# Holding activation loads back, under a new stored order, so that the first weights have the DMA engines alone, in a linear-attention plus gated-MLP kernel

## Chip, cores, metric

One core of one Trainium2 chip. The metric is device microseconds of one execution, median over the runs of a comparison, in which the kernel before runs on the same chip in the same rounds. The record calls an execution slow when a lower granted clock goes with a longer time, or when it is over 1.5% above the fastest of its kernel. Each trace is one execution.

## The reference

```python
h   = x + A(layernorm(x))          # linear attention: qkv = x @ wqkv, phi(q), phi(k), kv, o = num / den, o @ wo
h2  = h + B(layernorm(h))          # gelu(x @ w_in) in halves z1, z2; w_sp mixes layernorm(z2) over tokens; (z1 * g) @ w_out
# S = 2048 tokens (16 tiles of 128), D = 512, 32 heads; w_sp is 2048 x 2048; everything bf16
```

Mostly the opening matters here: layernorm of x by tiles of 128 tokens, transposition of the normalised tile (xn to xnT), the key product, the feature map (written pk), and the accumulation of pk with xn over all tokens. Later the normalised h (hn) is transposed by the DMA to hnT. In the profiles PE is TensorE, DVE is VectorE, ACT is ScalarE, POOL is GpSimd and SP is SyncE; a q behind the name (SPq) is the queue from which that engine issues its DMA transfers.

## The kernel before

The kernel records every operation with its dependencies and then emits them per engine in a **stored order** (`ORDER`, a packed list). The stored order decides how instructions stand on every engine; waits follow from the data.

```python
    x0 = load_x("SP", 0, 1, 2150)
    load_x("ACT", 1, 1, 2250)
    x2 = load_x("SP", 2, 1, 2500)
    load_x("ACT", 3, 1, 2500)
    wk = [first_load(eng, wqkv[:, c:c + 2, D:2 * D], ..., f"wk{c}", 3500)      # key weights, 2 x 256 KB
          for eng, c in (("SP", 0), ("ACT", 2))]
    for n, lat, behind in ((4, 3900, None), (6, 3500, x0), (8, 3600, x2), (10, 3300, wk[0]), (12, 3500, wk[0]),
                           (14, 3700, wk[0])):
        load_x("SP", n, 2, lat, behind)                                        # 256 KB each; behind = wait for that load
    first_load("SP", wqkv[:, :, 0:D], A_wqkv[:, 0:D], "wq", 4500)              # query weights, 512 KB
    # ... cut ...
    # tiles 0 to 5 are transposed by TensorE (HEAD = 6), tiles 6 to 15 by the DMA from SP:
            if n < HEAD:
                pe_transposes(xn[:, i, :], b + i % 2, xnT, i, second)
            else:
                g.last = dma_t(xnT[:, :, i * P:(i + 1) * P], xn[:, i, :], f"xt{i}")
                if i == HEAD:
                    first_xt = g.last
    # ... cut: w_sp, loaded transposed from HBM. The first of its tiles (EARLY = 1) goes ahead of all the xnT transposes:
        w = NT // 2 if EARLY <= i < NT // 2 else NT
        for j in range(0, NT, w):
            op = dma_t(wsp[:, j:j + w, t * P:(t + 1) * P], B_w_sp[...], ...)
            op.soft.add(queue["SP"][-1].i if i < EARLY else prev.i)
            prev = op if i >= EARLY else prev
            if i < EARLY:
                first_xt.soft.add(op.i)
```

So SP's queue reads: x0, x2, wk, x4 to x14, wq, one transposed w_sp load (512 KB), then the xnT transposes. No w_sp tile is used before about 120 us.

Of the kernel before, what the change touches and what calls it, by code (L numbers as in the profile page):

```python
# [11 lines left out]
P = 128  # L12
GRAN = 16
EARLY = 1
SEM_NS = 45.0
ORDER = "c-jrogMttU00qE@tj)G<d$VoZwz=81ZQHhO+jiZ}FH8U;Aqt`)I$|IuVj(u-pq}C*0RSQ#Lc$1!;0TQ{2mv8HA|f)PA}*335t1S?k|8-#ASH4k4{{?fQXwDmqYx^h0Mep7Dxm@zp$Xz4AyT6-(x3=3pdiwr7&0L}0+A6#kr|EA6qQj0&Cnbz(E?SG1zC{|HIN;}(G}fM0zJ?TB~cAIP#rZ<8*NYvtxyVeP#0rR8f7pJV=*4}P#;UM6wA;SIZ+nn&>pSP4n5Heeb5`B5CLH^0TVF^lhGdo&=>tM1s%`;4KWA<F%5&!5zEmD2XP385riQ)f)!YaRalLqIEE8Aj^P-Abr^{?IE_&ljj5Q9&gg=fn1T6NfLS<+g;<ZZIE6EKhUa*R7kG-<n1i7hh7H(=MOchY*n#cXj4hapdDw%!*oj@(jdM7Qeb|o!*otkqiYqve3%H0&xQWZShFiFf8+eUZc!RgNjeEF{JGhGn2+oHH!H|r=06s!QzQcPw#uNO+Cw#yUe8gvb!7qHpH^ks~{6S3q`@g)t8Ym1yF)Twf79%qfqcAGtF*f5e4#P7Xe<Ky6F*P$Y53?{j^D;jRFb&f(9n&)dGcps+tRxFEA4{<`|3b{h?99QO3}hh|W)T);E(T*w)?ryDU^&KTLM~wo7Gnw4Wi2LR875|VR$xU|VoTOzZB}L#)@K7YWFt1_V&>)=u4QZXVs}<$b+%z|E@fM`ViPuF4>nYBmSl1!WfCT13Z`Uo?co-tP*3h<A1>n*4rOY!V|#YsKCa__PGw3pWi{4db2d^MrP6vH;4pS%CoX4Su3$fQ<py?Uf3D;J4&)#PF}*S<tuiZ}wlbrpa|APKII}3LvTGZ&DW`HMmvSqwy0EcEas~&p8;7uonyQ(atA$#smGUT`@~fZ<sE`6xSfe<NGg(B%bcRJ$Ld8`|C3TjiRYpg6ly`WAcX^C&SWZ{@gxC0%<yBTs`G<e`j9>Vb-?*KlxskKDgF88!b2yjtxQSypmg6{{tGJ5?xsVe$pVxVuhj@dNc#rRRj^}xwhk28?c$=Gff+zW&7x;nCd5RzTf-m`r-}#UK_v!(E@F5p*0Vi`JE2)CQtD+*PvRW&d+NiDCsl7U=qdKXxx~PhRD}(~{nX9>*5%rT7`HQdkn~x|x=4n<_JXKXl#a9j0RCOiLYhGd~MN&dtW;8`tBE^suT45Ack(F3U6h*-lQ?Zm(;S^P|6-RN^Uv*SVGqg&*)kgy~NK-UeGgVhXnysPgs^RLU?pmu68mQG8qG1}Pahk4?nyT^Yrw!_%zUrxITBie=pt+i*(dwmn8l(AIpoJQ%Ihv?RO5({{qNQ4-Wm>O|+N{OeqHU_J<=U<_+N7;op_SU9ojRx#-m4SZrG473BRZ<%I;oUCrFcH9LprV9+M_f2pks>fq&}y!I<H*5pi8=<)K1{*x~6o#sLQ&etGcUOx~Y50?Sy`ykNT|p`lMt|<VSj_w0^8-dZHIf<yU&G41TKTdZ{n^s&{&;^!}#r`k};5<1EhVU;3$x{;hxdBl@rMI=O>6o9#@7<<Jh}0uJdA4(rSg=kU(&07r0kM|2biI+`Onvhz5HV>qYtIjW;OjtjZ43%aO_IHpUun2Wov>$#yDxuj#ev75N5OS`#yx|f@|tjoBCd%M2-x`F$+rCYhb`?<B-xUC0xpa*%d%ejJsJk&$n&J|tB<z3lTT-~KS!BsuclU>7;T+_8&&9&X$9o*5w-N~KZ#ob-UQ#{qvJj@%t$(udWBRtD9Jl&(c#oav0<2=?gy~eXW$Md|_>pa&ByvR$u-t)cCi@ns#z09k;(%Zb<JG|336w1N<UT+lFU42_y9m``p-aWj*E4<pf{2yF?$Zh"


class _Op:
# [13 lines left out]
class _Prog:  # L33
# [110 lines left out]
    def schedule(self):  # L144

        ids = np.frombuffer(zlib.decompress(base64.b85decode(ORDER)), np.uint16).tolist()
        assert len(ids) == len(self.ops)
# [105 lines left out]
def bass_sequential_preLN__linear_attn_block__mixer_gmlp__prompt_kernel(  # L253
# [11 lines left out]
    _, S, D = A_x.shape  # L265
    F = B_w_in.shape[1]
    FH = F // 2
    H = 32
# [9 lines left out]
    g = _Prog(nc)  # L278
# [37 lines left out]
    TB, SB = HT * GW * 2, HT * P * 2  # L316
# [3 lines left out]
    x = g.sbuf("x", o_x, [NT, D], BF16)  # L320
    h = g.sbuf("h", o_x, [NT, D], BF16)
    xn = g.sbuf("xn", o_xn, [NT, D], BF16)
    wqkv = g.sbuf("wqkv", o_wqkv, [KD, 3 * D], BF16)
# [19 lines left out]
    m = g.sbuf("m", o_m, [KD, D], BF16)  # L343
# [125 lines left out]
    wq = A_wqkv.rearrange("(c p) f -> p c f", p=P)  # L469
    queue = {"SP": [], "ACT": []}  # L470

    def load(eng, dst, src, nm, lat, issue=500.0):
        return dma(eng, dst, src.rearrange("(c p) f -> p c f", p=P), nm, lat=lat, issue=issue)

    def first_load(eng, dst, src, nm, lat, behind=None):
        q = queue[eng]
        op = load(eng, dst, src, nm, lat)
        op.bias = 1e6
        if q:
            op.soft.add(q[-1].i)  # L480
        if behind is not None:
            op.deps.add(behind.i)
        q.append(op)
        return op

    def load_x(eng, n, w, lat, behind=None):
        return first_load(eng, x[:, n:n + w, :], x_d[n * P:(n + w) * P, :], f"x{n}", lat, behind)
# [4 lines that stand above are left out]
    load_x("ACT", 3, 1, 2500)  # L492
    wk = [first_load(eng, wqkv[:, c:c + 2, D:2 * D], A_wqkv[c * P:(c + 2) * P, D:2 * D], f"wk{c}", 3500)
          for eng, c in (("SP", 0), ("ACT", 2))]
    for n, lat, behind in ((4, 3900, None), (6, 3500, x0), (8, 3600, x2), (10, 3300, wk[0]), (12, 3500, wk[0]),
                           (14, 3700, wk[0])):
        load_x("SP", n, 2, lat, behind)
    first_load("SP", wqkv[:, :, 0:D], A_wqkv[:, 0:D], "wq", 4500)
    exp_table = g.add("ACT", lambda ac: ac.preload_act_table_set("natural_log_exp_and_others"), [], [], cost=1300)
    exp_table.soft.add(queue["ACT"][-1].i)  # L500
    exps = []
# [104 lines left out]
    def next_pair():  # L606
        pc[0] += 1
        return PAIRS[pc[0] % 2]
# [118 lines left out]
    for c in range(KD):  # L727
        b = CB[1 - c % 2]
# [15 lines left out]
    for tg in range(NG):  # L744
# [12 lines left out]
        if tg not in MERGE:  # L757
# [3 lines left out]
            for t in range(first, tg + 1):  # L761
                for c in range(0, KD, 2):
                    q, r = pqT[:, c:c + 2, t * GW:(t + 1) * GW], r16[t // 2][:, c:c + 2, t % 2, :]
# [8 lines left out]
    for n in range(NT):  # L772
        b = AB[n % 3]
        matmuls(bank(b), [(pqT[:, c, n * P:(n + 1) * P], m[:, c, :]) for c in range(KD)])
        s = st[1][:, n, :]
# [20 lines left out]
    for n in range(NT):  # L796
        b = next_pair()
# [12 lines left out]
        s = st3[:, n, :]  # L810
# [18 lines left out]
    k = 0  # L829
    for tg in range(NG):  # L830
        for fc in range(KF):
            b = Z1B[k % 2]
# [6 lines left out]
    for i, t in enumerate(order):  # L839
        w = NT // 2 if EARLY <= i < NT // 2 else NT  # L840
# [12 lines left out]
    v1, v2, v3, v4 = (rows(0, HF, hi, half) for hi in (0, 1) for half in (0, 1))  # L853
# [166 lines left out]
```

## Time and profile before

| | |
|---|---|
| median | 233.85 us (3 runs, 233.68 to 233.93) |
| TensorE (PE) | busy 224.1 of 232.1 us, 89% of the chain that ended last |
| where PE is idle | mostly the first 19 us, some between 48 and 67 us |
| key weights | issued at 1.72, landed 5.8 us later |
| w_sp load | issued at 9.49, landed 8.5 us later, at 17.96 |
| first xnT by DMA | issued at 14.70, landed 3.8 us later, at 18.5 |

The page of the kernel before, its first part and its chain:

```profile
span 232.1 us, 3230 instructions
PE 224.1 (97%) x1180; PEld 110.4 (48%) x1203; DVE 159.8 (69%) x323; ACT 103.8 (45%) x193; POOL 45.0 (19%) x134
...
PE 89%; DVE 3%; DMA 3%; POOL 2%; issue 1%; ACT 1%; SPq 1%; DVEq 0%
```

PE bounds the kernel, and so anything that moves its dense stretch moves the end. The chain of waits of the kernel before, cut to the opening (start us, us, what):

```profile
2.19 6.07 DMA x<-in_A_x_dram
...
8.29 0.69 DVE st L511
8.98 0.64 DVE xn L556 x2
...
16.25 1.29 PE psum L655 x6
17.54 0.05 issue
17.60 1.24 PE psum L655 x5
18.84 1.73 PE psum L402 x8
```

The chain waits 6.07 us for x4, then passes through VectorE; from 12.9 us on it stays on PE. The timeline of the kernel before (start us, us, engine, line, operation, out<-in, count, and the idle time before with its releaser):

```profile
6.40 0.41 DVE L556 TENSOR_SCALAR xn<-x,st,rs 128x512 bf16<-128x512 bf16 x1 [0.31 <-ACT rs L421]
8.29 0.69 DVE L511 BATCH_NORM_STATS2 st<-x 128x6 f32<-128x512 bf16 x1 [1.47 <-DMA x<-in_A_x_dram]
8.90 0.72 DVE L556 TENSOR_SCALAR xn<-x,st,rs 128x512 bf16<-128x512 bf16 x2
...
9.91 2.75 PE L402 MATMUL psum<-wqkv,xnT 128*128 128x512 bf16 x12
...
18.68 1.89 PE L402 MATMUL psum<-wqkv,xnT 128*128 128x512 bf16 x8
20.40 1.89 PE L655 MATMUL psum<-pk,xn 128*128 128x512 bf16 x8
...
8.98 0.47 SPq L432 DMA_DIRECT2D wqkv<-in_A_wqkv_dram  x1
9.49 4.94 SPq L435 DMA_TRANSPOSE wsp<-in_B_w_sp_dram  x1
```

Two norms (8.90) wait for x4 only because the statistics of x4 stand in front of them on VectorE. The products at 18.68 are those of tiles 6 and 7, the first that use an xnT made by the DMA; the products of pk and xn at 20.40 (L655) are called the next group below. The DMA view of the kernel before (bytes of one issue, us from issue to landing):

```profile
wqkv<-in_A_wqkv_dram SPq DMA_DIRECT2D x1, 256.0 KB, 5.8
x<-in_A_x_dram SPq DMA_DIRECT2D x1, 256.0 KB, 6.1
...
wqkv<-in_A_wqkv_dram SPq DMA_DIRECT2D x1, 512.0 KB, 5.6
wsp<-in_B_w_sp_dram SPq DMA_TRANSPOSE x1, 8.5
...
xnT<-xn SPq DMA_TRANSPOSE x1, 3.8
```

The table of windows of the kernel before (stretch, us, busy time of each engine, granted clock, DMA share, GB/s):

```profile
2.00:9.00 7.00, 5.13 (x54) 4.12 (x53) 3.69 (x10) 4.78 (x12) 2.18 (x8) 1.00 0.84 262
9.00:17.00 8.00, 7.40 (x45) 3.38 (x46) 7.97 (x24) 6.32 (x11) 3.63 (x10) 1.00 1.12 243
```

The DMA share is the time of all packets over that of the 16 engines (packets that overlap can bring it above 1): 0.84 from 2 to 9 us and 1.12 from 9 to 17 us; by single microseconds it is 0.34 from 8 to 9 us.

### The profile page before, as it was taken

The numbers are of one execution on the slowest core, as the hardware profiler recorded it, in microseconds if no ns is written. First come the engines' busy times: TensorE is split into PE (matmuls) and PEld (weight loads), VectorE is DVE, ScalarE is ACT, GpSimd is POOL, SyncE is SP. The second block draws the span as 40 slices with busy tenths as digits, with TensorE's granted clock in tenths as the row PEclk, the third lists the DMA queues.
The fourth block names the chain that finished last, engine by engine and source line by source line (L and its number), as shares of the span: only waits on it lengthen the run. The fifth ranks groups of instructions, "written<-read, shape, count | busy, mean of one in ns | idle before, by whom it ended". The sixth has DMA issues, their size and how long they took to land.

```text
span 232.1 us, 3230 instructions
## 1 busy us (share of the span) xinstructions
PE 224.1 (97%) x1180; PEld 110.4 (48%) x1203; DVE 159.8 (69%) x323; ACT 103.8 (45%) x193; POOL 45.0 (19%) x134
## 2 busy tenths in 40 slices
PE   7699999999999999999999999999999999999995
PEld 7344444453344443455444444444455555555453
DVE  3699855637898820129679996688797695582595
ACT  5586654389869687689762010112111212013110
POOL 3354300000665500726851000000000000000000
PEclk9999999999999999999999999999999999999999
DMA  6894339937457469939999300000000002000015
GB/s 189 262 206 91 57 60 336 340 72 182 110 98 156 95 131 146 186 78 212 176 226 222 73 3 0 0 0 0 3 0 24 0 3 90 0 24 3 0 45 181
DMA packets 58864, 23.68 MB, mean 102 GB/s; under 512 B 48480, under 2 KB 58720, under 8 KB 58848
## 3 DMA queue, kind: packets, MB, share of 16 engines
q1 hardware_dynamic: 58144, 22.88, 44.8%
q10 hardware_dynamic: 704, 0.59, 0.8%
q8 instruction: 9, 0.15, 0.3%
q14 instruction: 7, 0.06, 0.1%
HBM read 7.47 MB, written 2.10 MB: 41 GB/s over the span
## 4 chain that ended last, share of the span: by engine, by line
PE 89%; DVE 3%; DMA 3%; POOL 2%; issue 1%; ACT 1%; SPq 1%; DVEq 0%
PE psum L402 70%; PE psum L655 6%; PE psum L802 6%; PE psum L805 4%; DMA x<-in_A_x_dram 3%; DVE st L511 1%; POOL rs L551 1%; PE psum L751 1%; SPq L432 1%; ACT m L421 0%; POOL st L535 0%; PE psum L720 0%; PE psum L676 0%; DVE xn L556 0%; PE psum L685 0%
## 5 line engine op out<-in xcount | busy, mean ns | idle before, releaser
L421 ACT ACTIVATE psum<-psum 128x256 f32<-128x256 f32 (+1 forms) x33 | 14.4, 445 | 91.6 <-PE psum L402 42.5
L402 PE MATMUL psum<-wsp,z 128*128 128x512 bf16 x203 | 47.1, 379 | 0.3
L402 PEld LDWEIGHTS psum<-wsp,z 128*128 128x128 bf16 x208 | 20.3, 98 | 23.1 <-ACT psum L421 0.5
L402 PE MATMUL psum<-hnT,win 128*128 128x512 bf16 x109 | 25.3, 379 | 0.2
L402 PE MATMUL psum<-t,s 128*128 128x512 bf16 x94 | 22.2, 379 | 0.1
L421 ACT ACTIVATE e<-psum 128x1024 bf16<-128x1024 f32 (+1 forms) x18 | 16.7, 927 | 12.5 <-PE psum L402 12.0
L421 ACT ACTIVATE z1T<-psum 128x512 bf16<-128x512 f32 x28 | 16.3, 594 | 4.9 <-PE psum L402 4.9
L924 DVE TENSOR_TENSOR u<-psum,bsp 128x512 bf16<-128x512 f32 x16 | 11.0, 687 | 10.2 <-PE psum L402 7.5
L421 ACT ACTIVATE z<-psum 128x896 bf16<-128x896 f32 x16 | 14.5, 914 | 4.1 <-PE psum L805 4.1
L402 PEld LDWEIGHTS psum<-hnT,win 128*128 128x128 bf16 x112 | 9.9, 98 | 13.5 <-ACT z1T L421 4.1
L402 PE MATMUL psum<-wout,z1T 128*128 128x256 bf16 (+1 forms) x82 | 16.3, 314 | 0.0
L802 PE MATMUL psum<-win,hnT 128*128 128x512 bf16 x63 | 16.2, 379 | 0.1
L402 PE MATMUL psum<-wqkv,xnT 128*128 128x512 bf16 x62 | 14.9, 379 | 0.9 <-ACT xnT L421 0.8
L556 DVE TENSOR_SCALAR hn<-h,st,rs 128x512 bf16<-128x512 bf16 x16 | 6.0, 407 | 13.7 <-POOL rs L547 13.2
L402 PE MATMUL psum<-xnT,wqkv 128*128 128x512 bf16 x61 | 15.1, 379 | 0.2
L655 PE MATMUL psum<-pk,xn 128*128 128x512 bf16 x63 | 15.2, 379 | 0.1
L402 PE MATMUL psum<-m,pqT 128*128 128x512 bf16 x62 | 14.7, 379 | 0.4 <-DVE h L776 0.3
L402 PEld LDWEIGHTS psum<-t,s 128*128 128x128 bf16 x96 | 9.4, 98 | 10.4
L511 DVE BATCH_NORM_STATS2 st<-x 128x6 f32<-128x512 bf16 x15 | 9.9, 677 | 5.0 <-DMA x<-in_A_x_dram 5.0
L776 DVE SCALAR_TENSOR_TENSOR h<-psum,x 128x512 bf16<-128x512 f32 x16 | 10.5, 682 | 4.0 <-PE psum L402 4.0
L805 PE MATMUL psum<-win,hnT 128*128 128x384 bf16 x64 | 13.0, 326 | 0.0
L582 DVE TENSOR_SCALAR e<-e 128x1024 bf16<-128x1024 bf16 (+1 forms) x18 | 7.0, 391 | 7.9 <-ACT e L421 7.7
(113 smaller groups left out, 348.6 us busy)
## 6 DMA issues: line engine op xcount, KB each, us to landing
r<-rcp SPq DMA_DIRECT2D x16, 128.0 KB, 2.7
out_dram<-h SPq DMA_DIRECT2D x15, 128.0 KB, 1.8
win<-in_B_w_in_dram SPq DMA_DIRECT2D x2, 896.0 KB, 8.6
x<-in_A_x_dram SPq DMA_DIRECT2D x6, 256.0 KB, 4.8
wqkv<-in_A_wqkv_dram SPq DMA_DIRECT2D x2, 512.0 KB, 8.6
wout<-in_B_w_out_dram SPq DMA_DIRECT2D x1, 896.0 KB, 8.0
wo<-in_A_wo_dram SPq DMA_DIRECT2D x1, 512.0 KB, 4.1
bsp<-in_B_b_sp_dram SPq DMA_DIRECT2D x1, 512.0 KB, 4.8
```

The source lines that it names most:

```text
L402: inst = pe.matmul(out_ap, lhsT=a, rhs=b, start=start and i == 0, stop=stop and i == len(pairs) - 1, **kw)
L421: return g.add("ACT", lambda ac: ac.activation(out_ap, in_ap, func, **kw), [in_ap, *extra], [out_ap] + ([accum] if accum is not None else []),
L432: return g.add(eng, lambda q: q.dma_start(out_ap, in_ap), [in_ap], [out_ap], cost=issue, lat=lat, dma=name, **k)
L511: dve(lambda v: v.bn_stats(s[:, 0:6], src[:, n, :]), [src[:, n, :]], [s[:, 0:6]], D)
L551: pool(lambda p: p.tensor_tensor(r, ve, expo[:, 0:1], ALU.pow), [ve, expo], [r], 620)
L556: return dve(lambda v: v.tensor_scalar(dst, src, mean, rst, op0=ALU.subtract, op1=ALU.mult), [src, mean, rst], [dst], w + 460, acc=4)
L582: dve(lambda v: v.tensor_scalar(e, e, 1.0, EPS_PHI, op0=ALU.min, op1=ALU.add), [e], [e], w * GW, acc=4)
L655: inst = pe.matmul(bank(CB[c]), lhsT=xn[:, i, c * P:(c + 1) * P], rhs=pk[:, i, :], start=i == 0, stop=i == NT - 1)
L776: dve(lambda v, n=n, b=b, s=s: v.scalar_tensor_tensor(h[:, n, :], bank(b), 1.0, x[:, n, :], op0=ALU.mult, op1=ALU.add, accum_out=s[:, 0:1] ...
L802: pe.matmul(bank(b), lhsT=hnT[:, c, n * P:(n + 1) * P], rhs=win2[:, c, 0:GW], start=c == 0, stop=c == KD - 1)
L805: inst = pe.matmul(bank(b + 1, F2), lhsT=hnT[:, c, n * P:(n + 1) * P], rhs=win2[:, c, GW:FH], start=c == 0, stop=c == KD - 1)
L924: dve(lambda v: v.tensor_tensor(t, bank(b), add, ALU.add), [bank(b), add], [t], GW, ps=True)
```

## The change

Intent: x4 and x6 wait for the landing of x2, and x8 to x14 for that of the key weights, so that the key weights do not share the DMA engines. The stored order was made anew for the new arrival times, so every engine's order differs.

```diff
-ORDER = "c-jrogMttU00qE@tj)G<d$VoZwz=81ZQHhO+jiZ}... (cut)"
+ORDER = "c-jTQ17HvU00h8Cwq47%ZQHhO+qGrewr$(CZ5wwH5gA... (cut)"
...
-    for n, lat, behind in ((4, 3900, None), (6, 3500, x0), (8, 3600, x2), (10, 3300, wk[0]), (12, 3500, wk[0]),
-                           (14, 3700, wk[0])):
+    for n, lat, behind in ((4, 2000, x2), (6, 2200, x2), (8, 1900, wk[0]), (10, 2100, wk[0]), (12, 2300, wk[0]),
+                           (14, 2500, wk[0])):
         load_x("SP", n, 2, lat, behind)
-    first_load("SP", wqkv[:, :, 0:D], A_wqkv[:, 0:D], "wq", 4500)
+    first_load("SP", wqkv[:, :, 0:D], A_wqkv[:, 0:D], "wq", 3400)
```

The change has two parts: **the hold** (the `behind` entries; the latencies are only estimates of the scheduler and change no instruction) and **the schedule** (`ORDER`).

More of the change, by code (lines that the diff above doesn't have):

```diff
@@ L15 @@
 SEM_NS = 45.0
-ORDER = "c-jrogMttU00qE@tj)G<d$VoZwz=81ZQHhO+jiZ}FH8U;Aqt`)I$|IuVj(u-pq}C*0RSQ#Lc$1!;0TQ{2mv8HA|f)PA}*335t1S?k|8-#ASH4k4{{?fQXwDmqYx^h0Mep7Dxm@zp$Xz4AyT6-(x3=3pdiwr7&0L}0+A6#kr|EA6qQj0&Cnbz(E?SG1zC{|HIN;}(G}fM0zJ?TB~cAIP#rZ<8*NYvtxyVeP#0rR8f7pJV=*4}P#;UM6wA;SIZ+nn&>pSP4n5Heeb5`B5CLH^0TVF^lhGdo&=>tM1s%`;4KWA<F%5&!5zEmD2XP385riQ)f)!YaRalLqIEE8Aj^P-Abr^{?IE_&ljj5Q9&gg=fn1T6NfLS<+g;<ZZIE6EKhUa*R7kG-<n1i7hh7H(=MOchY*n#cXj4hapdDw%!*oj@(jdM7Qeb|o!*otkqiYqve3%H0&xQWZShFiFf8+eUZc!RgNjeEF{JGhGn2+oHH!H|r=06s!QzQcPw#uNO+Cw#yUe8gvb!7qHpH^ks~{6S3q`@g)t8Ym1yF)Twf79%qfqcAGtF*f5e4#P7Xe<Ky6F*P$Y53?{j^D;jRFb&f(9n&)dGcps+tRxFEA4{<`|3b{h?99QO3}hh|W)T);E(T*w)?ryDU^&KTLM~wo7Gnw4Wi2LR875|VR$xU|VoTOzZB}L#)@K7YWFt1_V&>)=u4QZXVs}<$b+%z|E@fM`ViPuF4>nYBmSl1!WfCT13Z`Uo?co-tP*3h<A1>n*4rOY!V|#YsKCa__PGw3pWi{4db2d^MrP6vH;4pS%CoX4Su3$fQ<py?Uf3D;J4&)#PF}*S<tuiZ}wlbrpa|APKII}3LvTGZ&DW`HMmvSqwy0EcEas~&p8;7uonyQ(atA$#smGUT`@~fZ<sE`6xSfe<NGg(B%bcRJ$Ld8`|C3TjiRYpg6ly`WAcX^C&SWZ{@gxC0%<yBTs`G<e`j9>Vb-?*KlxskKDgF88!b2yjtxQSypmg6{{tGJ5?xsVe$pVxVuhj@dNc#rRRj^}xwhk28?c$=Gff+zW&7x;nCd5RzTf-m`r-}#UK_v!(E@F5p*0Vi`JE2)CQtD+*PvRW&d+NiDCsl7U=qdKXxx~PhRD}(~{nX9>*5%rT7`HQdkn~x|x=4n<_JXKXl#a9j0RCOiLYhGd~MN&dtW;8`tBE^suT45Ack(F3U6h*-lQ?Zm(;S^P|6-RN^Uv*SVGqg&*)kgy~NK-UeGgVhXnysPgs^RLU?pmu68mQG8qG1}Pahk4?nyT^Yrw!_%zUrxITBie=pt+i*(dwmn8l(AIpoJQ%Ihv?RO5({{qNQ4-Wm>O|+N{OeqHU_J<=U<_+N7;op_SU9ojRx#-m4SZrG473BRZ<%I;oUCrFcH9LprV9+M_f2pks>fq&}y!I<H*5pi8=<)K1{*x~6o#sLQ&etGcUOx~Y50?Sy`ykNT|p`lMt|<VSj_w0^8-dZHIf<yU&G41TKTdZ{n^s&{&;^!}#r`k};5<1EhVU;3$x{;hxdBl@rMI=O>6o9#@7<<Jh}0uJdA4(rSg=kU(&07r0kM|2biI+`Onvhz5HV>qYtIjW;OjtjZ43%aO_IHpUun2Wov>$#yDxuj#ev75N5OS`#yx|f@|tjoBCd%M2-x`F$+rCYhb`?<B-xUC0xpa*%d%ejJsJk&$n&J|tB<z3lTT-~KS!BsuclU>7;T+_8&&9&X$9o*5w-N~KZ#ob-UQ#{qvJj@%t$(udWBRtD9Jl&(c#oav0<2=?gy~eXW$Md|_>pa&ByvR$u-t)cCi@ns#z09k;(%Zb<JG|336w1N<UT+lFU42_y9m``p-aWj*E4<pf{2yF?$Zh"
@@ new lines @@
+ORDER = "c-jTQ17HvU00h8Cwq47%ZQHhO+qGrewr$(CZ5wwH5gAbt9Wf9Su@D<^5Eu2800D@ED2Rr5$b~$}jl4*LqyUHz2nE3iiC_qhWJrz_NQp#9j8w>n{3w9JNQ(-ngvO|hifD@XNQl%(gMui6bjW~0NROh(gp4SL;;4eE$c!dvhAgOttSEtOsEO>Tj&A6I?kI_#D23)|fpBPrmgt4v=!-tcfm*16wy2FdXpPdSi+UJ`GAN7sXn-*oi}6^7B{+=bSc-PYiE=294rqh+XoyA_fPol{e&~-u=!i}@g3dUILzsYxn1sn#foYh6Ay|pf2#+ubi&cn#)i{b{IDz9BieU)ENCaUNMq>@uVLGOw3%X(^W?%v4<1|iU78YVH*5eGG;uKz@fg0)sp5qy2V-AL61U6tJ7GW`VU^_NpGqzwZ=3x)^VkdTCH_qWK_F+E`U@Nxa3a;WjF5n_A;U+HQ8gAh_Zr~N(;5FXjHtypN?&2OEA~+u)1Vi#2BJdF+G7{h8F`nQjKHvvF;uk*QAHLu-zTqprBPPMH49!ps!&o$9Gb*DoGNUja<1-H9G91J6H)1dqQ!@`UGdlA!3-hx8(=aX5F+DRdBQvoaOS2ZqeEfr~EJ*P$$}kwSF*|cGCkwGWb1{GkSeQjvl*L$=3Au#z*pj)~gSA<lCE13Fn3xr~m}Oa?OIe4l*qXiBmVH=}l~|co*p6$smJQgDjaZfK*^@Qcm`&J=eVLTWS%RgQgvq#t$(4dlnUc-9hbgp-TbWvEG@MgdjoUbaBiWA~*pZ#sp99#L138Gxxt%+>f-5<d={22=)L1pSjx(4+d%2HY*p1EDg4LN)sgzl1704hC<zRMaR}SM4Hc=L(Q$~$qCQai^o?%vHQ+DN0PUTiE<y9W#S3VU`K^0aZ713E9VR02z2^CXml~fs(S1Fa%9UkQ|-sKg(;Z>H?6TW2y&EkF@;6bkE25#hNj^S92<4*44A&%#4&f#3H;yg~^ah~9OF63cO;wEn9J>KU7KIBQB;yb?Q2cF}3Uf@OU=4r0xHD2c>HdQk<R|~aND^2DCPUIq1RAp7tA3o(X{$&+a)fawcHHBAeB~u%<RXep;2X#~@bygR3RRn!waD`A!g;Xtl<a6HOO+MlazT_>w;wS!NL|x`<J|+}NRAhbU5B}sY-e!CyP!xqyXh~rdRbgcXD4~8ckrFG3s;h>gD~3KZreZ0!!YP`PDvshRnBr-G`e?9ftFC6Kj%I3zhN_+hs;_2ixVmYIrfQJ7tG{|^l~!w-rYle*HCMybQzO(*qclz%G+MnBr16@ddFrkC8lzd7sC8PPC0eMpO5(Aaqyw6xrCOuOTBh~dsLfiWE!wJs+NPvltP@(U?b@Xk+N71*p}jh+L)xvK+Nb?GqCGmQ<4Wk0I;GP(qeMQY#LnfjI;RvquM4`QD@y5$itl8;rcb)A54x<Yx}&?grJK5^+`g{|O6>#=@JBt;L#6U#J<|(4(Nm@MXT8=drE_{e*B8CiS7q=!z125;*AFFk7XQ*uW%O_T6a7bjmEXZ^!*XbcabAaX2#0lehjSWda#m+{HWzR~M{q<(avn!@WJh-t7jkw-a|{=DKF4t^$8-+obP*SIF_&>!7k3HQbA88kBR6&vH*hmIbxD_ULr-!GH+OlrbSw9A8~1h}w{}IBb|qK#1o!hq_jP{{a67kkdk^#=5AiTp@nBbVIoEInS95jObS>9*M|bu{*Ku8UcMnhTR8MmUZ}Mgj^(+r}Cy(?DPxlsg@np|*kViPsvpvsqJl6}n$V)um3%%G&J<g-u)nmQfqrA+kywYpD*6SSG!F@yV+|!}F)$jF2x7E#KyxJ=~-s`==+q~U7ywkh<AMVe{ZU"
```

## The prediction

> **What bounds the kernel now.** TensorE: busy 224.1 of 232.1 us (first part of the page), 89% of the chain that ended last, granted clock 1.00. Its idle time lies almost wholly in the first 19 us and between 48 and 67 us (timeline of PE, table of windows).
>
> In the opening the chain of waits reads: x load until 8.29 us, statistics of x4 on VectorE, then norms. The x4 load was issued at 2.19 and took 6.1 us to land; the key weights, issued at 1.72, took 5.8 to 6.0 (landing 7.5 to 7.8); x8, issued near 4.06, took 5.6. So 0.5 MB of weights shares the DMA engines with up to 0.75 MB of x not needed yet. The Trainium skill (DMA: Bandwidth & Descriptors, "Two DMAs through the same engine are not ordered") says descriptors start in order but are pipelined; the trace agrees that being early in the queue did not land the weights quickly.
>
> The weights are not the tight wait, though: the first key product is released at 7.83 by ScalarE's copy of xnT. What costs most is VectorE's order: the statistics of x4 stand before the norms of x3 and x1, which so wait until 8.98, although their inputs were ready by about 7.2. TensorE idles for it at 7.27 to 7.86, 8.89 to 9.35, 12.66 to 12.91.
>
> **What changes.** x4 and x6 wait for x2 (landed about 4.06), x8 to x14 for the first key weights. No bytes or arithmetic are added. The stored schedule is replaced whole: in the opening the norms of tiles 0 to 3 come before the statistics of x4, and PE does 16 transposes, then 16 key products unbroken. Late weights are reordered (wo last), the kvm product moves ahead of the second normaliser, the tail is reordered.
>
> **Costs, walked by hand with traced durations.** Most of the first 1 MB moves before x4 starts (29, 307, 242, 270 KB in the microseconds from 1 to 5), so the key weights land about 6.3 instead of 7.6, x4 about 7.0, x8 about 8.8. Norms (0.40 each) at 5.7, 6.4, 6.8, 7.2; xnT copies (0.59) end by 9.0; key products (0.216) run from about 8.0 to 11.5, against 12.66 now. VectorE then carries the stage: the fourth pk is done at 16.9 instead of 17.6. The transposed w_sp load starts about 0.8 earlier (9.49 now), and with it the first DMA-transposed xnT lands about 17.7 for 18.5. The dense stretch that starts at 18.84 should start near 18.1: 0.7 us gained, all on the critical path, since PE has almost no slack afterwards. Between 49 and 57 us the wo products lose about 0.4 us waiting for copies; the new interleaving may save 0.2. The rest I call neutral, plus or minus 0.5.
>
> **Prediction.** 233.0 us, 8 in 10 between 232.2 and 233.9. Faster by over 2%: 0.01; within 2%: 0.98; slower by over 2%: 0.01.
>
> **What would show it.** Key weights landing near 6.3 us (4.5 from issue, not 5.9); no VectorE wait for x4 over 0.5 us; 16 unbroken key products ending by 11.6; products of tiles 6 and 7 starting near 18.1; PE busy time still near 224; PE idle 0.5 to 1 us less.
>
> **What would make it wrong.** x4 or x6 landing after 8 us, so that VectorE waits again; the w_sp transposed load not starting earlier; wo, now last, landing after about 51.5 us and stalling the m products; a tail whose last adds and stores end later after the last product than today's 3.3 us.

## The result

233.54 us median (233.13 to 234.12, 6 runs) against 233.89 us for the kernel before in the same rounds (233.35 to 234.48): ratio 0.9985, 95% interval 0.9962 to 1.0009. Ratios here are the mean time of one kernel's fast runs over that of the other's of the same rounds, so not quite the ratio of the medians quoted. Later with five rounds (experiment e9): 0.9988, interval 0.9968 to 1.0007. The best estimate is a gain of 0.3 to 0.5 us, and neither comparison excludes zero.

The page of the changed kernel:

```profile
span 231.8 us, 3231 instructions
PE 224.6 (97%) x1180; PEld 112.1 (48%) x1203; DVE 161.6 (70%) x323; ACT 104.3 (45%) x193; POOL 44.2 (19%) x134
...
PE 86%; DMA 6%; ACT 3%; DVE 2%; issue 1%; SPq 0%
```

DMA has risen from 3 to 6% of the chain: something new is being waited for. The chain of waits of the changed kernel, cut to the opening:

```profile
4.00 3.56 DMA x<-in_A_x_dram
...
7.58 1.88 DVE st L511 x3
...
13.70 0.70 ACT xn L421
14.40 0.07 ACT e L421
14.47 4.06 DMA xnT<-xn
18.53 0.05 issue
18.58 0.61 PE psum L402 x2
```

The last wait is the new one: 4.06 us for the first xnT. The timeline of the changed kernel:

```profile
6.27 1.06 DVE L556 TENSOR_SCALAR xn<-x,st,rs 128x512 bf16<-128x512 bf16 x3 [0.31 <-ACT rs L421]
7.58 1.88 DVE L511 BATCH_NORM_STATS2 st<-x 128x6 f32<-128x512 bf16 x3 [0.25 <-DMA x<-in_A_x_dram]
...
7.90 3.52 PE L402 MATMUL psum<-wqkv,xnT 128*128 128x512 bf16 x15
...
14.63 2.75 PE L655 MATMUL psum<-pk,xn 128*128 128x512 bf16 x12
18.58 1.90 PE L402 MATMUL psum<-wqkv,xnT 128*128 128x512 bf16 x7 [1.20 <-DMA xnT<-xn]
20.32 1.89 PE L655 MATMUL psum<-pk,xn 128*128 128x512 bf16 x8
...
8.35 0.47 SPq L432 DMA_DIRECT2D wqkv<-in_A_wqkv_dram  x1
8.86 5.56 SPq L435 DMA_TRANSPOSE wsp<-in_B_w_sp_dram  x1
```

The opening did what it was meant to do. The norms no longer wait for x4, the key products run unbroken and end at 11.42 instead of 12.66 us, and PE begins the products of pk and xn at 14.63 instead of 16.09. Then PE stands still for 1.20 us, and the next group starts at 20.32 against 20.40: of the 1.46 us, 0.08 is left. The DMA view and the windows of the changed kernel:

```profile
wqkv<-in_A_wqkv_dram SPq DMA_DIRECT2D x1, 256.0 KB, 4.7
...
x<-in_A_x_dram SPq DMA_DIRECT2D x1, 256.0 KB, 3.6
...
wqkv<-in_A_wqkv_dram SPq DMA_DIRECT2D x1, 512.0 KB, 6.2
wsp<-in_B_w_sp_dram SPq DMA_TRANSPOSE x1, 9.1
...
xnT<-xn SPq DMA_TRANSPOSE x1, 4.1
```

```profile
2.00:9.00 7.00, 6.88 (x64) 6.06 (x64) 5.04 (x13) 5.60 (x14) 1.39 (x5) 1.00 0.85 262
9.00:17.00 8.00, 7.93 (x43) 3.40 (x41) 7.93 (x23) 6.85 (x12) 3.88 (x11) 1.00 1.09 243
```

The key weights land 1.1 us sooner. But the rates, 262 and 243 GB/s, are those of before to the digit: the same bytes in the same time. The query weights, the last plain load ahead of w_sp, are issued 0.63 us earlier (8.35 for 8.98) and land at 14.54 in both traces. So w_sp, which also starts 0.63 us earlier, lands at 17.98 instead of 17.96, in both 3.4 us after the query weights. (Landings to two digits here are those of the packed trace; the views round them to 0.1.)

### The profile page after: what moved, and what is told of

It reads as the page before. It is cut to its first block, busy times and chain, and to the rows that moved or that the text cites. A ratio compares the mean times of both kernels' runs of the same rounds, so it can differ in the third digit from the quotient of the medians.

```text
span 231.8 us, 3231 instructions
## 1 busy us (share of the span) xinstructions
PE 224.6 (97%) x1180; PEld 112.1 (48%) x1203; DVE 161.6 (70%) x323; ACT 104.3 (45%) x193; POOL 44.2 (19%) x134
## 4 chain that ended last, share of the span: by engine, by line
PE 86%; DMA 6%; ACT 3%; DVE 2%; issue 1%; SPq 0%
PE psum L402 70%; PE psum L802 6%; PE psum L655 5%; PE psum L805 4%; DMA x<-in_A_x_dram 3%; DMA xnT<-xn 2%; DMA hnT<-hn 1%; DVE st L511 1%; ACT sh L421 1%; ACT xn L421 1%; ACT e L421 0%; ACT xnT L421 0%; PE psum L751 0%; PE psum L676 0%; PE psum L720 0%
## 5 line engine op out<-in xcount | busy, mean ns | idle before, releaser
L802 PE MATMUL psum<-win,hnT 128*128 128x512 bf16 x64 | 16.4, 379 | 0.4 <-DMA hnT<-hn 0.4
L776 DVE SCALAR_TENSOR_TENSOR h<-psum,x 128x512 bf16<-128x512 f32 x16 | 10.8, 688 | 5.2 <-PE psum L402 5.1
L402 PEld LDWEIGHTS psum<-t,s 128*128 128x128 bf16 x96 | 9.4, 98 | 10.3
L556 DVE TENSOR_SCALAR z<-z,st,rs 128x896 bf16<-128x896 bf16 x16 | 7.2, 493 | 7.3 <-POOL rs L519 7.3
```

The source lines that it names most:

```text
L402: inst = pe.matmul(out_ap, lhsT=a, rhs=b, start=start and i == 0, stop=stop and i == len(pairs) - 1, **kw)
L556: return dve(lambda v: v.tensor_scalar(dst, src, mean, rst, op0=ALU.subtract, op1=ALU.mult), [src, mean, rst], [dst], w + 460, acc=4)
L776: dve(lambda v, n=n, b=b, s=s: v.scalar_tensor_tensor(h[:, n, :], bank(b), 1.0, x[:, n, :], op0=ALU.mult, op1=ALU.add, accum_out=s[:, 0:1] ...
L802: pe.matmul(bank(b), lhsT=hnT[:, c, n * P:(n + 1) * P], rhs=win2[:, c, 0:GW], start=c == 0, stop=c == KD - 1)
```

## The experiments

Theory Q: the first xnT cannot land until the w_sp load ahead of it is through, and that is set by the bytes queued ahead on busy engines, not by the order in which the x tiles and key weights arrive. Rivals: the hold alone makes what gain there is (H); the hold buys nothing anywhere (N); the wait is really for ScalarE (S); a later stage takes gains back (L); the transposed load costs a fixed stall (F), or its own time (I), whatever stands ahead.

### e1 and e10: the hold alone

```diff
 (the changed kernel, with the stored order of before)
-ORDER = "c-jTQ17HvU00h8Cwq47%..."
+ORDER = "c-jrogMttU00qE@tj)G<..."
```

> The new load waits with the old stored schedule. Theory Q (the first DMA-transposed xnT tile cannot land before the w_sp transposed load that stands ahead of it in SP's queue is through, near 18.0 us in both kernels, whatever happens before): key weights land near 6.5 as in the changed kernel, x4 near 7.6, the 16th key product a little earlier than 12.66 us, but the first product of tiles 6 and 7 still starts at 18.4 to 18.9 us and the time is within 0.15 us of before. Rival H (the hold itself makes the gain and the schedule only follows): 0.25 us or more faster than before, products of tile 7 starting 0.3 us or more earlier.

Measured: 234.42 us against 233.59 for before, ratio 1.0035 (1.0023 to 1.0047). The profiled execution was the fastest of the six (233.78) and showed no loss: x4 landed at 7.7, but the next group started at 20.35, no sooner than before. Rival H is out. Slower was not expected by either theory, so the kernel ran again:

> The hold with the old schedule once more: its timed runs were 0.8 us slower than before although its profiled execution, the fastest of six, was level. If the slowness is real it comes again (ratio 1.002 to 1.005) and, if the profiled execution is now a typical one, the trace shows PE waiting longer than 0.3 us for the first transposed xnT (landing near 19), as theory Q would have it. If the ratio is now within 0.999 to 1.001, the first result was the chip's scatter and the hold alone is simply worth nothing.

It was run on another chip. Measured: 234.13 against 233.81, ratio 1.0027 (1.0006 to 1.0048): the loss is real. This time the profile caught the longest of the six (234.98 us). The timeline and the DMA view of e10:

```profile
8.97 6.75 SPq L435 DMA_TRANSPOSE wsp<-in_B_w_sp_dram  x1
...
19.82 1.47 PE L402 MATMUL psum<-wqkv,xnT 128*128 128x512 bf16 x6 [1.25 <-DMA xnT<-xn]
```

```profile
wsp<-in_B_w_sp_dram SPq DMA_TRANSPOSE x1, 10.3
```

The same program, a w_sp load of 10.3 us instead of 9.0, PE waiting 1.25 instead of 0.3 us, the next group 1.21 us later (21.56 for 20.35) and the execution 1.20 us longer (234.98 for 233.78). Between these two executions that one landing is the whole difference, and it is late because of what stands ahead: x14 landed at 14.42 for 13.05 and the query weights at 15.85 for 14.57, and w_sp followed them by 3.4 us in both.

### e2: the schedule alone

```diff
 (the kernel before, with the stored order of the changed kernel)
-ORDER = "c-jrogMttU00qE@tj)G<..."
+ORDER = "c-jTQ17HvU00h8Cwq47%..."
```

> The old load waits with the new stored schedule. Theory Q: the new order of VectorE alone gives the unbroken 16 key products (ending by about 12 us, since the norms no longer stand behind x4), PE then waits for the first transposed xnT as in the changed kernel; products of tile 7 start at 18.4 to 18.9; the stretch from 49 to 65 us gains about 0.2; time 0.15 to 0.35 us below before, the same as the changed kernel within 0.2. Rival H: no gain, or slower than before, since x4 lands at 8.3 and VectorE runs late.

Measured: 233.03 against 233.59, ratio 0.9979 (0.9961 to 0.9998). In its trace x4 lands at 8.2, the key products still run unbroken from 7.95 to 11.35, w_sp lands at 17.6, the products of tiles 6 and 7 start at 18.23 (18.4 to 18.9 was expected) and the next group at 19.97. The schedule alone is at least as good as the whole change (0.9985 and 0.9988). It beat the stated gain (0.15 to 0.35 us) by 0.2; the intervals of the two overlap, so no more than "not worse" is claimed.

### e3: the changed kernel with the first w_sp load late

```diff
+        for op, names in self.moved:               # in schedule(): edit the stored order
+            ids.remove(op)
+            at = max(k for k, i in enumerate(ids) if self.ops[i].dma in names)
+            ids.insert(at + 1, op)
...
             if i < EARLY:
-                first_xt.soft.add(op.i)
+                g.moved.append((op.i, [f"ht{i}" for i in range(NT)]))   # behind the last hnT transpose, ~100 us
```

> The changed kernel with the first w_sp transposed load moved from before the first xnT transpose to behind the last hnT transpose (about 103 us). Theory Q: the first xnT transpose is issued near 13.3 instead of 14.47 and lands by 16.5; PE's 1.2 us wait before tile 7 goes; the next product there starts at 17.3 to 17.5 us; if nothing later takes it back the time is 0.9 to 1.2 us below the changed kernel (232.3 to 232.7). Rival S (the wait is for ScalarE's norm of tiles 6 and 7, not for the queue): PE still waits to about 18.5, time within 0.2 of the changed kernel. Rival L (a later stage takes gains back): tile 7 starts by 17.5 but the time falls by less than 0.4 us.

Measured: 232.00 us (231.68 to 232.30) against 233.59, ratio 0.9931 (0.9919 to 0.9943). This beats both kernels, lies 0.3 us below the expected range and is the fastest version found. The timeline and the DMA view of e3 (lines moved by five in its listing):

```profile
14.39 2.75 PE L660 MATMUL psum<-pk,xn 128*128 128x512 bf16 x12
16.98 1.89 PE L407 MATMUL psum<-wqkv,xnT 128*128 128x512 bf16 x7
18.71 1.89 PE L660 MATMUL psum<-pk,xn 128*128 128x512 bf16 x8
...
13.00 1.44 SPq L440 DMA_TRANSPOSE xnT<-xn  x1
```

```profile
xnT<-xn SPq DMA_TRANSPOSE x1, 2.5
```

PE no longer waits: the first xnT is issued at 13.00, as soon as ScalarE has normalised it, and lands 2.5 us later. The group that began at 20.32 begins at 18.71, and the execution is 231.68 instead of 233.52: 1.6 us in the opening, 1.8 at the end (the other 0.2 is found below the tables). Rivals S and L are out.

### e4: the kernel before with the first w_sp load late

The same edit on the kernel before.

> The kernel before with the same move of the w_sp load. There PE was itself only ready for tile 7 at about 18.4, so theory Q expects a gain of 0.1 to 0.4 us only: the w_sp load and the opening's order bind at nearly the same time, so that each change alone gives little and both together about 1.2. If the gain here is as large as in the changed kernel (0.9 or more), the two do not interlock and theory Q's account of the opening is wrong.

Measured: 233.70 against 233.59, ratio 0.9997 (0.9984 to 1.0009): nothing. The next group starts at 20.25, since with the old schedule and no hold PE is itself not ready earlier. The expected 0.1 to 0.4 us was missed, if narrowly. The same w_sp load that costs the changed kernel about 1.3 us (0.9985 against 0.9931) costs this one nothing. Moved to 102.93 us, that load held SP for 1.96 us and landed 4.5 us after its issue, as it did within 0.1 us in e3, e5 and e6:

```profile
wsp<-in_B_w_sp_dram SPq DMA_TRANSPOSE x1, 4.5
```

So some 4 to 4.6 of the 8.5 and 9.1 us that it takes in the opening are not its own.

### e5 and e6: the schedule, and the hold, each with w_sp late

The edit of e3 on e2 and on e1.

> Experiment e3 without the hold: new stored schedule, old load waits, w_sp load behind the last hnT transpose. Theory Q+ (the hold is worth its planned 0.8 us only where the w_sp load no longer fixes the first transposed xnT): x4 lands near 8.2, so VectorE delivers xn4 and the first pk about 0.6 to 0.8 later than in e3; the product of tile 7 starts at 17.6 to 17.9 instead of 16.98; time 0.5 to 0.9 us above e3, about 232.6 to 232.9. Rival N (the hold buys nothing anywhere, the schedule all): within 0.2 us of e3.

Measured: 232.78 against 234.00, ratio 0.9944 (0.9923 to 0.9966), 0.8 us above e3 by medians but only 0.13% by ratios, from different rounds and chips, so the hold is worth 0.3 to 0.8 us here, and the intervals overlap. In its trace (its slowest run) the last of the key weights land at 8.25, PE waits 0.54 us for them, the products of tiles 6 and 7 start at 18.40 (17.6 to 17.9 was expected, 16.98 in e3) and the next group at 20.13, against 18.71 in e3.

> The old stored schedule with the hold and the late w_sp load (e4 plus the hold). From the trace of the hold alone, PE was ready for tile 7 at 18.1, with the w_sp load gone it should go on there: 0.4 us below before in the trace (about 233.1 to 233.3). Rival N: same as e4, within 0.15 of before. If it is slower than before by 0.5 or more, as the hold alone was in its timed runs, then the hold does harm that has nothing to do with w_sp.

Measured: 233.29 against 234.00, ratio 0.9970 (0.9951 to 0.9989); next group at 19.88 against 20.25 in e4, the 0.4 us expected. Without the w_sp load ahead the hold helps also the old schedule. Rival N fails on e6, whose interval excludes 1 where that of e4 does not: the hold does have worth, but only where its gain can reach PE. And the loss that the hold alone made is gone with w_sp late, so it came by way of that load.

### e7: only half of the w_sp load early

```diff
-        w = NT // 2 if EARLY <= i < NT // 2 else NT
+        w = NT // 2 if i < NT // 2 else NT
...
+            if i < EARLY and j:                    # second half: behind the last hnT transpose, as in e3
+                g.moved.append((op.i, [f"ht{i}" for i in range(NT)]))
+                continue
```

> The changed kernel with only half of the first w_sp load (8 of 16 blocks) ahead of the xnT transposes, the other half moved to where e3 has it. Theory Q: SP's issue time of that load and its landing both shrink, landing 16.3 to 16.9 instead of 18.0, first xnT about 0.5 us after it (16.8 to 17.4), so PE waits 0 to 0.3 us for tile 7 and most of e3's gain is there: 232.0 to 232.5. Rival F (a transposed load costs a fixed stall of the queue, whatever its size): landing near 17.5 or later, time within 0.4 us of the changed kernel.

Measured: 232.53 against 234.00, ratio 0.9936 (0.9918 to 0.9955). The load was issued at 9.15, held SP 2.94 us and landed 8.4 us later, at 17.5; the first xnT landed at 17.9 and PE waited 0.54 us. This lies between the two accounts: the time is nearly Q's, the landing nearly rival F's. The query weights ahead explain it: in this execution they landed at 14.98, 0.44 us later than in the changed kernel. The half load followed them by 2.54 us where the whole one took 3.44. So its size does count, against F in its pure form (a stall whatever the size); two sizes do not say how much of the rest is fixed.

### e8: the query weights moved behind the w_sp load

```diff
     first_load("SP", wqkv[:, :, 0:D], A_wqkv[:, 0:D], "wq", 3400)
+    g.moved.append((queue["SP"].pop().i, ["xt6", "xt7"]))   # behind the first two xnT transposes
```

> The changed kernel with the w_sp load where it was, but the query weights (512 KB) moved from ahead of it to behind the transposes of tiles 6 and 7. Theory Q as a matter of bytes in the queue: the w_sp load lands 1 to 1.7 us earlier (16.3 to 17.0), the first xnT near 17.0 to 17.5, time 0.6 to 1.2 us below the changed kernel, provided the query weights still land before their first use at 23.8. Rival I (it is the transposed load's own time, not what stands ahead): it starts 0.5 earlier and lands 0.5 earlier (17.5), gain at most 0.5 us.

Measured: 232.57 against 234.00, ratio 0.9948 (0.9926 to 0.9970). w_sp, untouched, was issued at 8.13, landed 7.8 us later, at 15.9, which is 2.1 us earlier; the first xnT landed at 16.4 and PE went on at 16.95 without a wait:

```profile
wsp<-in_B_w_sp_dram SPq DMA_TRANSPOSE x1, 7.8
```

Now x14 is the last plain load ahead; it landed at 12.48, and w_sp came 3.44 us after it, the same 3.44 us as after the query weights in the changed kernel. There x14 landed at 12.84 and the query weights 1.70 us later, so 1.7 of the 2.1 us are the query weights; the rest is that the x loads came sooner in this execution. Rival I (17.5) is out: it is what stands ahead that counts. Part of the gain goes again at 20.9, where the transposes of tiles 8 and 9 now sit behind the query weights and PE waits 0.34 us.

### e9: the changed kernel again, unedited

No edit; it was run to narrow the first comparison and to see how far its opening scatters.

> The changed kernel once more, unedited, with five rounds beside the kernel before, because its first comparison left an interval that holds zero. If the trace is right (PE 0.3 us ahead from 65 us on), the ratio is 0.998 to 0.9995. Its first transposed xnT should again land near 18.5 us and PE wait 0.9 to 1.4 us for it; if another execution shows it landing at 17.8 or before, the landing is not fixed by the w_sp load as theory Q says.

Measured: 233.29 us against 233.81, ratio 0.9988 (0.9968 to 1.0007). The interval again includes 1, so the gain stays a best estimate. w_sp was issued at 8.99 and landed at 17.6, the first xnT at 18.13, and PE waited 0.86 us for it, against 1.20 in the first profile (0.9 to 1.4 was expected): the wait and its releaser are there again, the size moves with the landing. The query weights had landed at 14.17 instead of 14.54, with the same program, so landings scatter by some 0.4 us from one execution to the next.

### The table of all of it

Ratio to the kernel before of the same rounds, by what was taken:

| | w_sp early | w_sp late |
|---|---|---|
| old schedule, no hold | 1 (before) | 0.9997 (e4) |
| old schedule, hold | 1.0035, 1.0027 (e1, e10) | 0.9970 (e6) |
| new schedule, no hold | 0.9979 (e2) | 0.9944 (e5) |
| new schedule, hold | 0.9985, 0.9988 (after, e9) | 0.9931 (e3) |

And from the profiled executions, the landing of w_sp, the landing of the first xnT, the start of the next group on PE, and what is left of the execution after that start:

| | w_sp lands | xnT lands | next group | rest |
|---|---|---|---|---|
| before | 17.96 | 18.5 | 20.40 | 213.47 |
| hold, e1 and e10 | 18.0, 19.3 | 18.6, 19.8 | 20.35, 21.56 | 213.43, 213.42 |
| e4, e6 (w_sp late) | | | 20.25, 19.88 | 213.43, 213.42 |
| after, e9 | 17.98, 17.6 | 18.5, 18.1 | 20.32, 19.91 | 213.20, 213.00 |
| schedule, e2 | 17.6 | 18.2 | 19.97 | 213.17 |
| e3, e5 (w_sp late) | | 15.5 (e3) | 18.71, 20.13 | 212.97, 212.95 |
| e7 | 17.5 | 17.9 | 19.67 | 212.96 |

The rest is the time of that execution less the start of the group (233.87 − 20.40 = 213.47). It falls into two groups, 213.4 to 213.5 for the old schedule and 213.0 to 213.2 for the new. So nearly the whole story is two terms: when the opening lets PE go, and a figure of the schedule. Within the new schedule that figure moves with one later wait: at about 65 us PE waits 0.38 and 0.36 us for hnT in the changed kernel and e2 (rest 213.2), 0.17 in e9 (213.0) and not at all in e3, e5 and e7 (213.0). (e8, with its second wait, is left out: 213.78.) Wherever w_sp stands ahead, xnT lands 0.4 to 0.6 us after it. And w_sp itself lands 3.41 to 3.45 us after the last plain load ahead of it in all seven traces that load it whole (before, after, e1, e2, e8, e9, e10), although those loads land anywhere from 12.48 (e8) to 15.85 (e10). That is theory Q in one number.

## Why the prediction was right or wrong

The measured 233.54 us lies in the stated range, and "within 2%" was right; but the forecast gain was about 0.85 us and 0.35 was measured (0.3 to 0.5 with the repetition). The range reached to 233.9, so no gain at all would have lain in it too; it tells little about the mechanism. Point by point:

- **Right, as long as w_sp stands ahead: the weights were not the tight wait, VectorE's order was.** The schedule alone (e2), in which the weights land as late as before, keeps the gain; the hold alone does not. With w_sp late it holds less: there the hold is worth 0.3 to 0.8 us (e5 against e3), and in the trace of e5, where the weights landed at 8.25, PE waited 0.54 us for them.
- **Right: the compute of the opening.** Key weights from 1.71 to 6.4 (forecast 6.3); key products ended at 11.42 (11.5); the fourth pk was done at 16.24 (16.9, so even better). x4 landed at 7.56 rather than 7.0, and x8 at 10.8 rather than 8.8; VectorE waited only 0.25 us, for x4.
- **The step that failed:** "The transposed w_sp load starts about 0.8 earlier (9.49 now), and with it the first DMA-transposed xnT lands about 17.7 for 18.5." It started 0.63 earlier and landed at the same time, and so did xnT (18.53). The term "0.7 us gained" measured 0.08 (20.40 to 20.32). I took the load's 8.5 us as its own and slid it forward. But the plain loads ahead of it came through at the same time, the query weights at 14.54 in both kernels, and w_sp landed 3.4 us after them; e8 shows that removing bytes ahead is what moves the landing. A hold reorders bytes; it removes none, and here it brought the early ones forward but not the last one.
- **Right in size by luck: the later stage.** "May save 0.2" was said of the wo products between 49 and 57 us. The rest after the opening did fall from 213.4 to 213.0–213.2, in the first comparison 0.27 of the 0.35 us gained, but elsewhere: from the products with sel (47.38 and 47.30) to the first with m (56.96 and 56.83) only 0.05 us is gained, and 0.15 from there to the first with win (65.29 and 65.01), where PE waits for h, and for pqT before and hnT after.
- **A check that came true for the wrong reason.** "PE idle 0.5 to 1 us less" was met (8.0 to 7.2 us), but the 50 warm-up products took 5.51 us instead of 4.49, which counts as busy, and a new idle of 1.20 us had appeared. Total idle time hid both.

The Trainium skill's sentence on pipelined descriptors (DMA: Bandwidth & Descriptors, "Two DMAs through the same engine are not ordered") agrees with what the key weights did: 5.8 us with x behind them, 4.7 without. What was needed as well stands in Perfetto Trace Analysis, "DMA Instruction — HWDGE (DVE, Sync)": the duration shown for a DMA instruction is the time that its issue takes, descriptor generation included, and the movement of the data is not in it. The traces agree: the same w_sp load occupied SP for 4.29 to 6.75 us in the opening and landed 7.8 to 10.3 us after its issue, against 1.96 to 2.12 and 4.5 to 4.6 us when it was moved to 101 to 103 us.

Left open: why the plain loads ahead of w_sp, although issued earlier, can come through later under the hold with the old schedule (1.0035 and 1.0027, and the trace of e10). In e10 the engines moved 222 GB/s from 9 to 17 us, where they moved 241 in e1 with the same program; that says where the time went, not why. Nor was it settled whether xnT must wait for w_sp to land or only for its descriptors to be fetched.

## What to carry to other kernels

Before pricing a reordering of loads, look at the DMA share up to the moment of the *last* transfer that the dense stretch waits for: where it was near 1 here, order decided only who came early, and the last one came when the bytes ahead of it were through. Then ask which of those bytes are not needed: here a load first used at about 120 us stood ahead of one needed at 17, and moving it turned a gain of 0.35 us into one of 1.6 (ratio 0.9985 to 0.9931). And vary two limits together: w_sp late gave nothing on the kernel before, the hold did harm by itself, and schedule, hold and w_sp late together gave 0.69%.

## What the Trainium skill lacked or had wrong

- DMA: Bandwidth & Descriptors, on DMA transposes: it gives no figure for how long a transpose is held up behind other loads of the same queue. Here the 512 KB w_sp load landed 3.4 us after the last plain load ahead of it in seven traced executions, and the first xnT 0.4 to 0.6 us after w_sp in eight (with the half load of e7): 3.4 to 4.6 us after its own issue, and 2.5 us after it with w_sp away.
- Perfetto Trace Analysis, "DMA Instruction — HWDGE (DVE, Sync)": it gives no figure for how long an issue can take. Here one 512 KB transposed load occupied SP for 4.29 to 6.75 us behind a backlog (5.56 in the changed kernel), half of it for 2.94, and the whole for 1.96 to 2.12 with only hnT transposes ahead (e3 to e6).
- TensorE: Matmul & The Clock Gate, Part 1, puts the step from the slow to the fast clock near 4 us of sustained products, give or take 500 ns. Here it scattered more. The same 50 warm-up products from 1.04 us on took 4.40 to 5.51 us: they started every 107 ns at first, and went over to every 56 ns after 3.1 to 4.7 us in six traces (3.2 in the kernel before). In the other six, the changed kernel's among them, all 50 stayed slow, to the last start at about 6.25 us, 5.2 us after the first, while the granted clock column stood at 1.00. In the changed kernel the first transpose began at 6.35 us although its input was ready at 5.96; no run shows whether that cost time at the end.
